# First pairs' queries and keys loaded in 96 rows of six tokens and turned on TensorE, with a bound on outstanding loads

## The chip, the core and the metric

The program runs on one core of a Trainium2 chip. It uses all five engines of the core: TensorE (PE in the profile, with its weight loads as PEld), VectorE (DVE), ScalarE (ACT), GpSimd (POOL) and SyncE (SP), which here only issues DMA transfers. The metric is the device time of one execution in microseconds. The kernel before takes 704.54 us (median of 3 runs, 704.47 to 704.87).

## The reference

Eight batches, eight heads, 576 tokens of 64 numbers. Attention has two parts that are added: one on sequences pooled by four (144 tokens), one local, in which a token sees those less than four places away. The result is the input of a gated feed-forward block.

```python
q_d, k_d, v_d = (mean over groups of 4 tokens)
out_up = repeat(softmax(q_d k_d^T / 8) v_d, 4)
scores = where(|i - j| < 4, q k^T / 8, -1e9)
x = out_up + softmax(scores) v              # to (8, 576, 512)
x_prev = x shifted by one token
xk = mu_k * x + (1 - mu_k) * x_prev         # and xr with mu_r
k = max(xk @ w_k, 0)                        # w_k 512 x 1024
v = k * k @ w_v                             # w_v 1024 x 512
out = sigmoid(xr @ w_r) * v                 # w_r 512 x 512
```

The weights come as 64-bit floats, all else as 32-bit floats.

## The kernel before, in words

**Attention** goes by pairs of heads: 32 pairs, four to a batch. Of a pair, queries and keys are loaded (`load_raw`, L328 to L338, four transfers each, of 32 partitions x 18 x 32 numbers, so runs of 32 numbers), values once for the pooled part (`load_v4`) and once as windows of 32 tokens for the local part (`load_windows`). `turn_q` (L372) and `turn_k` (L381) put the 64 numbers of each head on partitions with VectorE's 32x32 transpose, GpSimd pools by four (`pool_q`, `pool_k`, `pool_v` at L422), TensorE makes all scores of the pair in one PSUM tile `ps_a` of which there is one (`score_both`: `down_last`, `score_pe`, `down_pe`). Then follow maxima and sums on VectorE (L523 the pooled part's maximum, L466 or L472 the local one's), exponentials on ScalarE, normalising on GpSimd (L477, L492, L544), a turn of the local part on VectorE (`score_turn`, L497), its spreading into a block pattern `bd` on ScalarE (L503), a turn of the pooled part on TensorE (`down_turn`, L556 to L558, copied by L565), the products with the values (`av_pe`, L575 and L581), and the sum of both parts into the batch's tile `xt` (`av_out`, L611). From pair 5 on the products with the values of the pair before are issued in the middle of a pair's scores (`run_pe`).

**Feed-forward** goes by 18 chunks of 256 tokens. Of a chunk the two mixed inputs are made (`diff` L632, `mix_part` L643 or L647, `mix_add` L657), each split in a high part (L661) and a low part (`mix_low`, L666, tile `xkl` or `xrl`), since products run in float32r in three passes high x high, high x low, low x high. Then come `k_pe` (L674, eight blocks of 12 products), the square on ScalarE and its split (L679 to L693), `r_pe` (L704) and `v_pe` (L719). Chunks 0 and 1 need only batch 0, so pairs 0 to 3; chunk 2 is the first that needs batch 1, pairs 4 to 7.

**Weights.** Twenty blocks of 128 x 512 64-bit numbers are loaded (`fetch_weight`, L278, 512 KB each) and made into 32-bit ones: one step on ScalarE (`weight_scale`, L283), three on VectorE (L287, L291, L296), a high part on ScalarE (L301) and a low part, of the first eight by TensorE (L307, L308) and ScalarE (L318), of the other twelve on GpSimd (`weight_low`, L323). Their order is k0 to k3, v0 to v3, k4 to k7, v4 to v7, r0 to r3.

**Order.** A planner (`Plan`) is given every task with its engine, a cost, a rank and the tiles it reads and writes; it walks through time with these costs and writes down an order for each engine, which the program then holds to. SyncE's loads are tasks like others, in one order, on one queue. The planner also puts filler products (`keep_warm`, L314, tile `ps_x`, results unused) where it expects TensorE to wait, up to a planned time `WARM1`. A load's end is counted on one of eight semaphores that take turns, so that a load waits for the end of the eighth-last one whatever else it waits for.

Of the kernel before, what the change touches and what calls it, by code (L numbers as in the profile page):

```python
# [32 lines left out]
SPLIT = 8  # L33
PEM = 4
# [10 lines left out]
class Plan:  # L45
# [8 lines left out]
    WARM0, WARM1, FILLER = 5.0, 100.0, 0.24  # L54
# [36 lines left out]
    def order(self):  # L91
# [126 lines left out]
def attention_moe(ctx: ExitStack, tc, q, k, v, mu_k, mu_r, w_k, w_v, w_r, band, ident, out):  # L218
# [108 lines left out]

    def load_raw(n, nm):  # L328
        b, p = divmod(n, NP)
        src = {"q": q, "k": k}[nm]  # L330
        raw = wp.tile([P, 18, 32], F32, tag="raw", name=nm + "raw", bufs=4)
        for e in range(2):
            for dh in range(2):
                o = 64 * e + 32 * dh
                nc.sync.dma_start(  # L335
                    raw[o:o + 32],
                    src[b, 2 * p + e].rearrange("(c t) (g d) -> t c g d", t=32, g=2)[:, :, dh, :])
        st.setdefault(n, {})[nm + "raw"] = raw  # L338
# [35 lines left out]
    def turn_k(n):  # L374
# [12 lines left out]
        d["k4"] = [(h, kz[h, e, 3:579]) for e, h in enumerate((slice(0, 64), slice(64, P)))]  # L387

# [336 lines left out]
    def store_out(c, t):  # L725
# [5 lines left out]
                     xkl=2, xrh=1, xrl=1, kk=2, kh=4, kl=4, sig=3, att=1))  # L731
# [69 lines left out]
    def weight(i):  # L801
# [102 lines left out]
    for c in range(NCH):  # L904
        while n <= NP * (segs(c)[-1][0] + 1):
            if n < n1:
# [6 lines left out]
                else:  # L913
                    add("PE", 3.3 if n < SPLIT else 2.85, at_run[n], run_pe, n, **join(av_of(n - 1), s))
# [24 lines left out]
    for t in emitted:  # L939
        in_order(t["f"], *t["args"])  # L940
# [40 lines left out]
```

## Time and profile before

| | |
|---|---|
| median of 3 runs | 704.54 us |
| profiled execution, its own time | 705.88 us |
| its span, first to last instruction | 703.9 us |
| busy share of the span: PE, DVE, ACT, POOL | 96%, 66%, 62%, 43% |
| first product of the feed-forward part (L674) | 73.97 us after the span's start |
| PE busy from 200 to 600 us | 397.66 of 400 us |
| packets of all transfers | 221849, 62.21 MB |

The profile is one execution. Its page and views give busy time by engine, groups of instructions by source line with the idle time ahead of them and what ended it ("<-"), and the chain of work that ended last. SPq rows are SyncE issuing transfers: the row's length is the time to issue, including a wait for a free semaphore, not the transfer. PEclk is the granted TensorE clock, 1.00 being full. Line numbers L... of the kernel before are those of the listing above; the changed kernel's lines are some 10 to 45 higher.

### The profile page before, as it was taken

Reading aid. Unit: us, or ns where it says so; the run is one execution under the profiler, and the core shown is the slowest. Engines: PE = TensorE matmul, PEld = TensorE weight load, DVE = VectorE, ACT = ScalarE, POOL = GpSimd, SP = SyncE. Lnnn points to the kernel's source line nnn. Section 1 sums busy time; section 2 is a strip of 40 time slices with the busy share of each in tenths; the row PEclk is TensorE's granted clock in tenths of the full one; section 3 lists DMA queues with packets and bytes.
Section 4 is the critical chain, followed back from the end, with each engine's and each line's share of the span. In section 5 each row is a group of like instructions: output and inputs, shape, how many; then the busy total and the mean of one; then the engine's idle time right before and its main releaser. Section 6 shows DMA issues by size and latency. Waiting matters only on the chain.

```text
span 703.9 us, 18635 instructions
## 1 busy us (share of the span) xinstructions
PE 674.1 (96%) x7467; PEld 576.9 (82%) x7467; DVE 465.5 (66%) x855; ACT 439.3 (62%) x1095; POOL 303.3 (43%) x374
## 2 busy tenths in 40 slices
PE   7888977999999999999999999999999999999997
PEld 5565866888888888888888888888888888988986
DVE  4778987659965977498753996488748963555111
ACT  3557864777757765667665667585758575744432
POOL 5535898656453646345341555455544521000000
PEclk9999998999999999999999999999999999999999
DMA  8899997635353426242351364334351100000000
GB/s 149 181 197 273 221 148 132 124 79 116 68 114 75 107 56 128 54 93 44 87 87 52 59 115 88 88 77 104 71 101 40 53 2 31 1 30 31 1 32 31
DMA packets 221849, 62.21 MB, mean 88 GB/s; under 512 B 205122, under 2 KB 214594, under 8 KB 221762
## 3 DMA queue, kind: packets, MB, share of 16 engines
q1 hardware_dynamic: 221762, 61.01, 42.0%
q8 instruction: 59, 0.97, 0.6%
q14 instruction: 28, 0.23, 0.1%
HBM read 51.55 MB, written 9.44 MB: 87 GB/s over the span
## 4 chain that ended last, share of the span: by engine, by line
PE 69%; DVE 11%; ACT 5%; SPq 4%; POOL 4%; DMA 3%; issue 3%; DVEq 0%; POOLq 0%; ACTq 0%
PE ps_g L674 24%; PE acc L719 22%; PE ps_r L704 12%; PE ps_v L581 3%; SPq L335 3%; PE ps_a L449 2%; PE ps_v L575 2%; DMA v<-in_v_dram 1%; ACT ad L533 1%; ACT L533 1%; DVE ps_w L291 1%; PE ps_a L516 1%; DMA wv<-in_moe_w_v_dram 1%; DVE kl L693 1%; PE ps_a L509 1%
## 5 line engine op out<-in xcount | busy, mean ns | idle before, releaser
L674 PE MATMUL ps_g<-xkh,wk 128*128 128x256 f32 x1152 | 229.5, 285 | 2.9 <-ACT kk L679 2.0
L674 PEld LDWEIGHTS ps_g<-xkh,wk 128*128 128x128 f32 x1152 | 186.6, 190 | 11.4 <-ACT kk L679 4.9
L719 PE MATMUL acc<-wv,kh 128*128 128x512 f32 x576 | 181.2, 396 | 0.0
L674 PE MATMUL ps_g<-xkl,wk 128*128 128x256 f32 x576 | 162.6, 282 | 0.7 <-DVE xkl L666 0.7
L693 DVE TENSOR_TENSOR kl<-kk,kh 128x256 fp32r<-128x256 f32 x119 | 64.0, 538 | 118.0 <-ACT kh L686 110.8
L719 PEld LDWEIGHTS acc<-wv,kh 128*128 128x128 f32 x576 | 101.0, 189 | 18.9 <-issue 2.5
L674 PEld LDWEIGHTS ps_g<-xkl,wk 128*128 128x128 f32 x576 | 109.9, 191 | 3.9 <-DVE xkl L666 0.9
L719 PE MATMUL acc<-wv,kl 128*128 128x512 f32 x288 | 112.6, 391 | 0.1
L679 ACT ACTIVATE kk<-ps_g 128x256 f32<-128x256 f32 x144 | 54.5, 379 | 84.2 <-PE ps_g L674 77.9
L704 PE MATMUL ps_r<-wr,xrh 128*128 128x512 f32 x288 | 90.2, 394 | 1.7 <-POOL wr L323 1.4
L693 POOL TENSOR_TENSOR kl<-kk,kh 128x256 fp32r<-128x256 f32 x25 | 18.5, 742 | 124.2 <-PE acc L719 96.1
L719 PEld LDWEIGHTS acc<-wv,kl 128*128 128x128 f32 x288 | 54.1, 188 | 12.8 <-DVE kl L693 0.8
L686 ACT ACTIVATE kh<-kk 128x256 fp32r<-128x256 f32 x144 | 60.2, 418 | 4.6
L685 ACT ACTIVATE kk<-kk 128x256 f32<-128x256 f32 x144 | 60.1, 418 | 4.5
L704 PEld LDWEIGHTS ps_r<-wr,xrh 128*128 128x128 f32 x288 | 52.5, 188 | 12.4 <-POOL wr L323 1.8
L477 POOL TENSOR_TENSOR sm<-sm,mx 128x384 f32<-128x384 f32 x28 | 24.4, 873 | 83.1 <-DVE sd L539 60.6
L704 PE MATMUL ps_r<-wr,xrl 128*128 128x512 f32 x144 | 56.1, 390 | 0.0
L523 DVE TENSOR_REDUCE mxd<-ps_a 128x3 f32<-128x432 f32 x32 | 19.3, 604 | 48.8 <-PE ps_a L449 39.6
L422 POOL TENSOR_TENSOR v<-v 72x512 f32<-72x512 f32 x32 | 44.6, 1395 | 16.0 <-DMA v<-in_v_dram 15.8
L423 POOL TENSOR_TENSOR vd<-v 72x256 f32<-72x256 f32 x32 | 27.7, 866 | 51.0 <-PE ps_v L575 49.6
L413 POOL TENSOR_TENSOR tk<-kz 64x288 f32<-64x288 f32 (+1 forms) x56 | 41.9, 748 | 16.1 <-DVE kz L386 12.5
L533 ACT ACTIVATE ad<-ps_a,mxd 128x144 f32<-128x144 f32 x96 | 35.3, 376 | 20.3 <-DVE mxd L524 17.5
(106 smaller groups left out, 1212.5 us busy)
## 6 DMA issues: line engine op xcount, KB each, us to landing
vw<-in_v_dram SPq DMA_DIRECT2D x126, 96.0 KB
qraw<-in_q_dram SPq DMA_DIRECT2D x128, 72.0 KB
kraw<-in_k_dram SPq DMA_DIRECT2D x128, 72.0 KB
v<-in_v_dram SPq DMA_DIRECT2D x32, 288.0 KB
out_dram<-sig SPq DMA_DIRECT2D x36, 256.0 KB
wk<-in_moe_w_k_dram SPq DMA_DIRECT2D x8, 512.0 KB
wv<-in_moe_w_v_dram SPq DMA_DIRECT2D x8, 512.0 KB
wr<-in_moe_w_r_dram SPq DMA_DIRECT2D x4, 512.0 KB
```

The costliest lines, as they stand in the source:

```text
L413: nc.gpsimd.tensor_tensor(out=tk[h], in0=k4[:, :, 0:2], in1=k4[:, :, 2:4], op=ALU.add)
L422: eng.tensor_tensor(out=v4[:, :, 0:128], in0=v4[:, :, 0:128], in1=v4[:, :, 128:256], op=ALU.add)
L423: eng.tensor_tensor(out=vd, in0=v4[:, :, 0:64], in1=v4[:, :, 64:128], op=ALU.add)
L477: nc.gpsimd.tensor_tensor(out=s3, in0=s3, in1=mx[:, :, None].broadcast_to([P, 12, 32]), op=ALU.subtract)
L533: nc.scalar.activation(ad[:, t, :], ps[:, t, :], AF.Exp, scale=1.0 / 128, bias=mx[:, t:t + 1], accum_out=sd[:, t:t + 1])
L674: nc.tensor.matmul(ps, w_k_part(p, f, w), y[:, p, :], start=(m == 0), stop=(m == len(mm) - 1))
L679: nc.scalar.activation(kk, kq[c, f], AF.Relu)
L685: nc.scalar.activation(kk, kk, AF.Square)
L686: nc.scalar.activation(kh, kk, AF.Copy)
L693: eng.tensor_tensor(out=kl, in0=kk, in1=kh.bitcast(F32), op=ALU.subtract)
L704: nc.tensor.matmul(ps, y[:, p, P * t:P * t + P], ws[f"r{p}"][:, w, :], start=(m == 0), stop=(m == len(mm) - 1))
L719: nc.tensor.matmul(accs[c][t], x[:, P * t:P * t + P], ws[f"v{f}"][:, w, :], start=(f == 0 and m == 0), stop=(f == NF - 1 and m == 2))
```

## The change

- Queries and keys of pairs 0 to 3 (`n < LONG`) are loaded by two transfers each instead of four, into a tile of 96 partitions, six consecutive tokens on each, the two heads side by side (runs of 64 numbers). The tile lies in the buffers of the first chunks' `xkh` and `xkl`.
- These are turned on TensorE, six transposes of 96 x 128 for queries and six for keys (`turn_pe`), three to a PSUM bank, and each three copied out by one instruction, for queries on ScalarE, for keys on VectorE (`turn_copy`). VectorE's 32x32 transposes of these pairs go. Two new rings bound how many turns (`turn`) and weights (`slot`) are in the works.
- Until a planned time of 130, a load waits until all loads have ended that lie further back than some 4 planned microseconds of transfers (`landed_before`); the planner starts none more than 3 ahead of its transfers (`AHEAD`). Fillers are put in until 130 instead of 100.
- For pairs 5 to 7 scores and the products with the values of the pair before are two tasks, scores first.
- As costs and tasks differ, the planner's order differs on all engines in the first part of the program. After its first 500 or so of some 3300 rows TensorE's order is the same as before.

```diff
-    WARM0, WARM1, FILLER = 5.0, 100.0, 0.24
+    WARM0, WARM1, FILLER = 5.0, 130.0, 0.24
+    AHEAD = 3.0
+    QUEUE = 4.0
...
             s = max(ready_at[t["id"]], free.get(t["eng"], 0.0), held.get(t["lock"], 0.0))
+            if t["dma"]:
+                s = max(s, dma_free - self.AHEAD)
...
     def load_raw(n, nm):
         b, p = divmod(n, NP)
         src = {"q": q, "k": k}[nm]
+        if n < LONG:
+            raw = wp.tile([TP, TN, 2, D], F32, tag=early_home(nm), name=nm + "raw", bufs=2)
+            for e in range(2):
+                nc.sync.dma_start(raw[:, :, e, :], bass.AP(src.tensor, (b * H + 2 * p + e) * S * D,
+                                                           [[TN * D, TP], [D, TN], [1, D]]))
+            st.setdefault(n, {})[nm + "raw"] = raw
+            return
...
+    def turn_pe(n, nm, i):
+
+        raw, c0 = st[n][nm + "raw"], sum(HALF[:i])
+        ps = pp.tile([P, HALF[i], TP], F32, tag=plan.bank[f"t{nm}{n}.{i}"], name="ps_q", bufs=1)
+        for c in range(HALF[i]):
+            nc.tensor.transpose(ps[:, c, :], raw[:, c0 + c, :, :].rearrange("p e d -> p (e d)"), idn[0:TP, 0:TP])
+        st[n][nm + "turn", i] = ps
+
+    def turn_copy(n, nm, i):
+        d = st[n]
+        c0 = sum(HALF[:i])
+        to = qTs[n % 2][:, 0:576] if nm == "q" else kzs[n % 2][:, 0, 3:579]
+        to = to.rearrange("p (t c) -> p c t", c=TN)[:, c0:c0 + HALF[i], :]
+        if on_turn(nm, i) == "ACT":
+            nc.scalar.activation(to, d[nm + "turn", i], AF.Copy)
+        else:
+            nc.vector.tensor_copy(out=to, in_=d[nm + "turn", i])
...
-                    add("PE", 3.3 if n < SPLIT else 2.85, at_run[n], run_pe, n, **join(av_of(n - 1), s))
+                    if n < SPLIT:
+                        add("PE", 1.9, at_run[n], score_both, n, **s)
+                        add("PE", 1.6, at_run[n], av_pe, n - 1, **av_of(n - 1))
+                    else:
+                        add("PE", 2.85, at_run[n], run_pe, n, **join(av_of(n - 1), s))
...
+    def landed_before(t):
+
+        if plan.when[t["id"]][0] > plan.WARM1:
+            return None
+        work = 0.0
+        for x in reversed(sent):
+            work += x["dma"]
+            if work > plan.QUEUE:
+                return x["last"]
+        return None
...
+                if waits is not None and ins.engine == every[-1]:
+                    tc.add_manual_dep(ins, waits.name, mybir.DependencyInfo(
+                        mybir.DependencyClass.Sync, mybir.DependencyReason.DATA), reason="landed")
+                    waits = None
```

**SyncE, the first loads.** `qraw` and `kraw` are the tiles of queries and keys, `wk` blocks of the first weight, `vw` the windows of the values; DMAHW0 to DMAHW7 are the eight semaphores on which loads' ends are counted. Before, from the second weight block to the third:

```order
L278 DMA wk1_110<-in_moe_w_k_dram 128x1024 [waits DMAHW3_49]
L344 DMA v4_112<-in_v_dram 72x4x256 [waits DMAHW4_49]
L335 DMA qraw_115<-in_q_dram 32x18x32 [waits DMAHW5_49]
L335 DMA qraw_115<-in_q_dram 32x18x32 [waits DMAHW6_49]
L335 DMA qraw_115<-in_q_dram 32x18x32 [waits DMAHW7_49]
L335 DMA qraw_115<-in_q_dram 32x18x32 [waits DMAHW0_49]
L335 DMA kraw_126<-in_k_dram 32x18x32 [waits DMAHW1_49]
L335 DMA kraw_126<-in_k_dram 32x18x32 [waits DMAHW2_49]
L335 DMA kraw_126<-in_k_dram 32x18x32 [waits DMAHW3_49]
L335 DMA kraw_126<-in_k_dram 32x18x32 [waits DMAHW4_49]
L358 DMA vw_215<-in_v_dram 32x11x64 [waits DMAHW5_49]
L362 DMA vw_215<-in_v_dram 29x64 [waits DMAHW6_49,DVE_49]
```

and now:

```order
L288 DMA wk1_100<-in_moe_w_k_dram 128x1024 [waits DMAHW3_49]
L364 DMA v4_112<-in_v_dram 72x4x256 [waits DMAHW5_49,DMAHW0_49]
L347 DMA qraw_126<-in_q_dram 96x6x64 [waits DMAHW6_49,DMAHW1_49]
L347 DMA qraw_126<-in_q_dram 96x6x64 [waits DMAHW2_49]
L347 DMA kraw_140<-in_k_dram 96x6x64 [waits DMAHW7_49]
L347 DMA kraw_140<-in_k_dram 96x6x64 [waits DMAHW4_49]
L378 DMA vw_218<-in_v_dram 32x11x64 [waits DMAHW0_49]
L382 DMA vw_218<-in_v_dram 29x64 [waits DVE_49]
L378 DMA vw_218<-in_v_dram 32x12x64 x2
L378 DMA vw_218<-in_v_dram 32x12x64 [waits DMAHW1_49]
L288 DMA wk2_236<-in_moe_w_k_dram 128x1024 [waits DMAHW4_49,DMAHW2_49]
```

Eight issues for the second pair's queries and keys have become four, and rows name a second semaphore, that of a load which must have ended: the pair's queries now wait for the first weight block (DMAHW6), the third weight block for the pair's keys (DMAHW4).

**VectorE, around the first chunk's inputs.** `w32` is a weight in 32 bits, `xk32` the mixed input, `xkl` its low part, without which the first product of the chunk cannot run. Before:

```order
L287 TENSOR_SCALAR ps_w_985<-ps_w_985 128x512
L291 SCALAR_TENSOR_TENSOR ps_w_985<-wk6_532,ps_w_985 128x512
L296 SCALAR_TENSOR_TENSOR w32_1007<-wk6_532,ps_w_985 128x512
L287 TENSOR_SCALAR ps_w_995<-ps_w_995 128x512
L291 SCALAR_TENSOR_TENSOR ps_w_995<-wk7_536,ps_w_995 128x512
L296 SCALAR_TENSOR_TENSOR w32_1017<-wk7_536,ps_w_995 128x512
L657 TENSOR_TENSOR xk32_1010<-xk32_1010,xt_102 128x1024
L287 TENSOR_SCALAR ps_w_1005<-ps_w_1005 128x512
L291 SCALAR_TENSOR_TENSOR ps_w_1005<-wv4_609,ps_w_1005 128x512
L296 SCALAR_TENSOR_TENSOR w32_1033<-wv4_609,ps_w_1005 128x512
L666 TENSOR_TENSOR xkl_1036<-xk32_1010,xkh_1028 128x1024
L372 STREAM_TRANSPOSE qT0_76<-qraw_650 128x576
```

and now:

```order
L306 SCALAR_TENSOR_TENSOR w32_987<-wk5_781,ps_w_977 128x512
L297 TENSOR_SCALAR ps_w_981<-ps_w_981 128x512
L301 SCALAR_TENSOR_TENSOR ps_w_981<-wk6_799,ps_w_981 128x512
L392 STREAM_TRANSPOSE qT0_76<-qraw_954 128x576
L700 TENSOR_TENSOR xk32_989<-xk32_989,xt_102 128x1024
L306 SCALAR_TENSOR_TENSOR w32_1009<-wk6_799,ps_w_981 128x512
L401 STREAM_TRANSPOSE kz0_73<-kraw_970 128x576
L709 TENSOR_TENSOR xkl_1018<-xk32_989,xkh_1012 128x1024
L297 TENSOR_SCALAR ps_w_1007<-ps_w_1007 128x512
L700 TENSOR_TENSOR dx_979<-dx_979,xt_102 128x1024
L301 SCALAR_TENSOR_TENSOR ps_w_1007<-wk7_816,ps_w_1007 128x512
L306 SCALAR_TENSOR_TENSOR w32_1112<-wk7_816,ps_w_1007 128x512
```

Blocks wk7 and wv4 have moved behind `xkl`, and the turns of pair 4's queries and keys (`qT0`, `kz0`) from behind it to ahead of it.

**TensorE, pair 6 and the first gate product.** `ps_a` are scores, `ps_v` products with the values, `ps_r` the gate products `r_pe`, `ps_x` fillers. Before:

```order
L704 MATMUL ps_r<-wr_1559,xrh 128x512 x2
L704 MATMUL ps_r<-wr_1559,xrl 128x512
L704 MATMUL ps_r<-wr_1601,xrh 128x512 x2
L704 MATMUL ps_r<-wr_1601,xrl 128x512
L509 MATMUL ps_a<-kd,qd_69 128x144
L575 MATMUL ps_v<-adT,vd 64x144 x4
L581 MATMUL ps_v<-bd,vw 64x48 x24
L516 MATMUL ps_a<-kd,qd_69 64x144 x4
L454 MATMUL ps_a<-kz_73,qT_76 32x32 x48
L674 MATMUL ps_g<-xkh,wk_235 128x256
```

and now:

```order
L601 MATMUL ps_t<-idn,ad 72x2x16
L324 MATMUL ps_x<-nidn 128x512 x14
L552 MATMUL ps_a<-kd,qd_69 128x144
L497 MATMUL ps_a<-kz_73,qT_76 32x32 x48
L559 MATMUL ps_a<-kd,qd_69 64x144 x4
L618 MATMUL ps_v<-adT,vd 64x144 x4
L624 MATMUL ps_v<-bd,vw 64x48 x24
L747 MATMUL ps_r<-wr_1450,xrh 128x512 x2
L747 MATMUL ps_r<-wr_1450,xrl 128x512
L747 MATMUL ps_r<-wr_1608,xrh 128x512 x2
L747 MATMUL ps_r<-wr_1608,xrl 128x512
```

The scores of pair 6 now stand whole and ahead of pair 5's products with the values, both ahead of the gate products, and 14 fillers ahead of them.

More of the change, by code (lines that the diff above doesn't have):

```diff
@@ L33 @@
 SPLIT = 8
+LONG = 4
+SLOTS = 2
+TURNB = 2
+HALF = (3, 3)
+TP, TN = 96, 6
+TURNS = "AADD"
 PEM = 4
@@ L326, in attention_moe, with early_home @@
     st, xts = {}, {}
+    def early_home(nm):
+        return "xkh" if nm == "q" else "xkl"
     def load_raw(n, nm):
@@ L730, in attention_moe @@
     plan = Plan(dict(raw=4, v4=2, vw=3, kd=2, sm=2, ad=1, adT=1, at=1, up=2, vd=2, xt=2, f32tmp=2, xkh=2,
[L731 removed]
+                     xkl=2, xrh=1, xrl=1, kk=2, kh=4, kl=4, sig=3, att=1, slot=SLOTS, turn=TURNB))
     add = plan.add
@@ L758, in pair_scores @@
         if part == 0:
-            add("DVE", 0.77, R - 9, turn_q, n, r=[f"qraw{n}"], w=[f"qT{i}"])
+            if n < LONG:
+                for nm in "qk":
+                    for x in range(2):
+                        add("PE", 0.14 * HALF[x] + 0.1, R - 10, turn_pe, n, nm, x, r=[f"{nm}raw{n}", "idn"],
+                            new=[(f"t{nm}{n}.{x}", "bank"), (f"u{nm}{n}.{x}", "turn")])
+                for nm in "qk":
+                    for x in range(2):
+                        add(on_turn(nm, x), 0.18 * HALF[x] + 0.14, R - 9, turn_copy, n, nm, x, r=[f"t{nm}{n}.{x}", f"u{nm}{n}.{x}"],
+                            w=[f"{nm}T{i}" + (f".{x}" if 0 else "")])
+            else:
+                add("DVE", 0.77, R - 9, turn_q, n, r=[f"qraw{n}"], w=[f"qT{i}"])
             if SPLIT <= n < SPLIT + 2:
                 add("POOL", 0.5, R - 9, clear_plane, i, w=[f"kT{i}"])
-            add("DVE", 0.77 if n < SPLIT else 1.53, R - 8.5, turn_k, n, r=[f"kraw{n}"], w=[f"kT{i}"])
+            if n >= LONG:
+                add("DVE", 0.77 if n < SPLIT else 1.53, R - 8.5, turn_k, n, r=[f"kraw{n}"], w=[f"kT{i}"])
             add("POOL", 1.12, R - 7, pool_q, n, r=[f"qT{i}"], w=[f"qd.{i}"])
@@ L922, in attention_moe, with in_order @@
     emitted = plan.fill(plan.order(), keep_warm)
-    last = {}
-    def in_order(f, *args):
+    last, sent = {}, []
+    def landed_before(t):
[7 more added lines that the diff above has]
+        return None
+    def in_order(f, *args, waits=None):
         traced = nc.cur_bb.bb.instructions
@@ L939, in attention_moe @@
     for t in emitted:
-        in_order(t["f"], *t["args"])
+        if t["eng"] == "SP":
+            in_order(t["f"], *t["args"], waits=landed_before(t))
+            sent.append(dict(dma=t["dma"], last=last[every[-1]]))
+        else:
+            in_order(t["f"], *t["args"])
 _INS = ["q", "k", "v", "moe_mu_k", "moe_mu_r", "moe_w_k", "moe_w_v", "moe_w_r"]
```

14 lines of the change are left out of this document (10 added, 4 removed).

## The prediction

> **What bounds the kernel now.** I read the view by stages first: busy microseconds of each engine in stretches, granted clock, share of the sixteen DMA engines.
>
> ```profile
> core 0: us, PE busy (x) PEld busy (x) DVE busy (x) ACT busy (x) POOL busy (x), PEclk, DMA share, GB/s
> 0.00:20.00 20.00, 14.36 (x152) 9.92 (x153) 9.59 (x20) 7.63 (x19) 11.01 (x28) 1.00 0.81 150
> 20.00:40.00 20.00, 17.81 (x373) 12.53 (x372) 12.53 (x27) 8.69 (x27) 9.81 (x14) 1.00 0.84 164
> 40.00:60.00 20.00, 14.92 (x219) 9.89 (x217) 15.89 (x34) 12.37 (x35) 7.52 (x10) 1.00 1.07 233
> 60.00:80.00 20.00, 18.98 (x137) 15.46 (x138) 18.99 (x25) 16.93 (x35) 12.74 (x10) 0.91 1.04 293
> 80.00:100.00 20.00, 18.34 (x272) 15.77 (x273) 18.69 (x31) 16.93 (x47) 19.28 (x23) 1.00 1.14 153
> 100.00:120.00 20.00, 13.23 (x290) 10.28 (x289) 13.62 (x22) 8.39 (x25) 16.84 (x18) 0.90 0.76 121
> 120.00:140.00 20.00, 19.76 (x287) 17.39 (x279) 13.86 (x28) 14.43 (x36) 13.18 (x18) 0.93 0.66 133
> 200.00:600.00 400.00, 397.66 (x4497) 346.26 (x4489) 278.39 (x522) 262.65 (x662) 175.58 (x213) 1.00 0.36 75
> ```
>
> From 120 us on TensorE never stops (397.66 of 400 us), and there its order is the same in both kernels. So whatever moves the start of that part moves the end by as much. The start is another matter: TensorE's first product of the feed-forward part waits, and its busy time before that is largely filler:
>
> ```profile
> 63.52 10.53 PE L314 MATMUL ps_x<-nidn 128*128 128x512 f32 x43
> 75.01 0.38 PE L674 MATMUL ps_g<-xkl,wk 128*128 128x256 f32 x1 [0.69 <-DVE xkl L666]
> ```
>
> VectorE sets that start: 18.99 and 18.69 of 20 us busy from 60 to 100, but only 38.01 of the first 60. What it waits for stands in its groups up to 125 us (busy, mean ns | idle ahead, what ended it):
>
> ```profile
> L287 DVE TENSOR_SCALAR ps_w<-ps_w 128x512 int32<-128x512 int32 x20 | 13.8, 689 | 9.2 <-ACT ps_w L283 9.2
> L372 DVE STREAM_TRANSPOSE qT<-qraw 128x576 f32<-128x576 f32 x9 | 7.0, 776 | 6.1 <-DMA qraw<-in_q_dram 6.0
> L381 DVE STREAM_TRANSPOSE kz<-kraw 128x576 f32<-128x576 f32 x8 | 6.1, 764 | 1.2 <-DMA kraw<-in_k_dram 1.2
> L611 DVE TENSOR_TENSOR xt<-ps_v,up 128x288 f32<-128x288 f32 x12 | 4.8, 443 | 0.0
> L523 DVE TENSOR_REDUCE mxd<-ps_a 128x3 f32<-128x432 f32 x7 | 4.2, 604 | 8.0 <-PE ps_a L454 4.8 <-PE ps_a L516 3.2
> L497 DVE STREAM_TRANSPOSE at<-sm 128x384 f32<-128x384 f32 x6 | 3.4, 571 | 2.6 <-POOL sm L492 2.6
> ```
>
> The 9.2 us at L287 are weights that had not landed; two of the waits are
>
> ```profile
> 25.41 0.70 DVE L287 TENSOR_SCALAR ps_w<-ps_w 128x512 int32<-128x512 int32 x1 [3.86 <-ACT ps_w L283]
> 46.70 0.70 DVE L287 TENSOR_SCALAR ps_w<-ps_w 128x512 int32<-128x512 int32 x1 [2.03 <-ACT ps_w L283]
> ```
>
> Last the chain of waits over the first 145 us, by line, and the queue:
>
> ```profile
> by line: SPq L335 13.9%; issue 8.4%; DMA v<-in_v_dram 6.7%; DVE ps_w L291 4.2%; DMA wv<-in_moe_w_v_dram 4.1%; DVE ps_w L287 3.7%; DMA wk<-in_moe_w_k_dram 3.5%; SPq L358 3.1%; PE ps_g L674 2.8%; POOL v L422 2.6%; DMA vw<-in_v_dram 2.2%; POOL
> 1.64 2.04 SPq L335 DMA_DIRECT2D qraw<-in_q_dram  x4
> 3.73 2.12 SPq L335 DMA_DIRECT2D kraw<-in_k_dram  x4
> ```
>
> Issuing queries and keys (L335) is 13.9% of 145 us, 20 us, of the chain: more than any engine's work. So in the first 60 us loads bound, from 60 to 100 VectorE (with GpSimd at 19.28 of 20 from 80), then TensorE.
>
> **The change part by part**, each in microseconds of the end; the sum goes from the profiled execution's own 705.88.
>
> *Loads, +5.0.* A load of queries or keys takes SyncE 2.04 to 2.12 when nothing holds it, 0.52 an issue; with two issues 1.04. That is 4.2 less ahead of the weight awaited at 25.41 (four such loads) and 8.3 less ahead of the one awaited at 46.70 (eight). In packets the load goes from 2304 of 128 bytes to 1152 of 256.
>
> ```profile
> q1 hardware_dynamic: 221762, 61.01, 42.0%
> ```
>
> 42.0% of 16 engines over 703.9 us for 221762 packets is 21.3 ns each, at a mean of 275 bytes. If cost goes by packet, a load falls from 3.07 to 1.53 us of the sixteen engines, 12.3 for eight; if by byte, nothing. VectorE can win at most its 9.2 at L287, and nothing if the loads go by bytes and its own order keeps it waiting elsewhere (8.0 at L523 is for scores, which stays). I take 5.0: the 3.86 and 2.03, covered by 4.2 and 8.3, less one.
>
> By the Trainium skill ("DMA: Bandwidth & Descriptors", Why small descriptors are slow) a descriptor has an overhead of about 3 cycles beside one per 32 bytes: 7 cycles for 128 bytes, 11 for 256. By it, an estimate, a load keeps 79% of its engine time, nearer to the byte end than to the packet end.
>
> *First pair, +0.5.* The waits at L372 and L381 (7.3 in all) start the chain. Keys need 1.04 less of issuing in each of two loads, but turn and copy come between: six transposes at the pace of
>
> ```profile
> 19.07 0.30 PE L556 MATMUL ps_t<-idn,ad 128*72 128x128 f32 x1 [1.04 <-POOL ad L544]
> 19.64 0.26 PE L558 MATMUL ps_t<-idn,ad 128*72 128x32 f32 x2
> ```
>
> are 0.8, two copies 0.7 to 0.9 in place of a turn of 0.77. Bounds -0.5 to 1.5.
>
> *VectorE's work, +2.6.* Four turns of queries go, 4 x 0.776 = 3.1. Four of keys, 3.06, become eight copies from PSUM; nearest is L611, 288 numbers from PSUM in 0.443: 3.54. Net 2.6. The copies write with a stride of six; at twice the price it would be -0.9.
>
> *ScalarE, 0.* Eight copies like
>
> ```profile
> 43.45 0.41 ACT L565 ACTIVATE adT<-ps_t 72x288 f32<-72x288 f32 x1 [1.04 <-PE ps_t L558]
> ```
>
> are 3.3 us, hidden: ScalarE is busy 16.3 of the first 40. Without that cover, -3.3. TensorE's 48 transposes, about 6 us, stand where fillers did.
>
> *Pair 3's values, +1.0.* They land late, with GpSimd and then the turn waiting:
>
> ```profile
> 55.81 1.27 POOL L422 TENSOR_TENSOR v<-v 72x512 f32<-72x512 f32 x1 [1.90 <-DMA v<-in_v_dram]
> 58.71 0.58 DVE L497 STREAM_TRANSPOSE at<-sm 128x384 f32<-128x384 f32 x1 [1.29 <-POOL sm L492]
> ```
>
> With less ahead of them they come earlier; 0 to 1.3, I take 1.0.
>
> *Order, 0.* Blocks wk7 and wv4 go behind `xkl`: six steps, 6 x 0.69 = 4.1, off the first product, but owed to the weights after it; pair 4's two turns, 1.54, go ahead. That moves the first product, not the end. Splitting scores from the products with the values frees VectorE's wait at `ps_a L454`, up to 4.8; against it stand 18 fillers behind the first products, 18 x 0.245 (10.53 by 43) = 4.4, free only while TensorE waits there, which it does now (100 to 120: 6.77 idle). I take 0 of -4.4 to 4.8.
>
> *Landing waits, -1.5.* SyncE issues in order, so each holds all later loads. A wait costs what the loads in flight do not cover:
>
> ```profile
> 1.17 0.42 SPq L240 DMA_DIRECT2D idn<-in_ident_dram  x1
> 3.12 0.31 ACT L247 ACTIVATE nidn<-idn 128x128 fp32r<-128x128 f32 x1 [1.11 <-DMA idn<-in_ident_dram]
> 60.00:64.00 4.00, 3.67 (x53) 2.36 (x54) 3.69 (x7) 3.96 (x9) 0.20 (x1) 0.67 1.03 411
> ```
>
> From issue to use 1.95 us; a weight of 512 KB at 411 GB/s is 1.28. With one weight in flight the queue runs dry for 0.67, with two not at all. Most places keep two or three; the third weight block and the values behind it keep one. I take 1.5, of 0 to 0.67 for each of some 34 loads.
>
> **Sum.** 5.0 + 0.5 + 2.6 + 0 + 1.0 + 0 - 1.5 = 7.6: 705.88 becomes 698.3. The median lay 1.34 below that execution, so 696.9; I say 697. The first product should come at 75.0 - 7.6 - 4.1 + 1.5, about 65.
>
> **The rivals.**
>
> *More is won (692.5).* The idle 6.77 from 100 to 120 and the clock of 0.90 there also go: the split run lets scores pass and fillers keep the clock, 4.5 more. For it: the chain's 8.4% "issue". Against it: GpSimd is at 16.84 of 20 there, and the last weight's low part is late on it:
>
> ```profile
> 112.36 1.27 POOL L323 TENSOR_TENSOR wr<-w,wr 128x512 fp32r<-128x512 f32 x1
> ```
>
> *Given back at GpSimd (702).* Its work is not reduced, and at 19.28 of 20 it takes over: only VectorE's 2.6 remains at the end, though the first product comes early. Against it: GpSimd idles 7.26 from 60 to 80, so it too can start earlier.
>
> *Packets cost by the byte (701).* The change then does not do what it says: the loads' 5.0 fall to some 1 by SyncE alone. For it: the DMA share is 1.04 to 1.14 from 40 to 100. Against it: 0.81 and 0.84 in the first 40, where these loads are.
>
> *The landing waits starve the queue (709).* The place is SyncE's queue from the second weight on. If each of some 34 loads up to wv7 is late by 0.4, 13.6 is lost against 9.1 won, 4.5 slower; from 0.27 each it ends slower. Pair 4's queries are behind all these, and their turn now stands ahead of `xk32` on VectorE, so the first product would be held directly. Against it: loads waited before too, for the eighth-last, and that covers little less for runs of small ones. The Trainium skill's same page (Anatomy of one DMA) puts the fixed cost of a transfer near 2 us, most of it the receipt after the last byte, written for transfers that GpSimd issues; the 1.95 here agrees, and it is the reason why a wait for the landing is dear.
>
> **How the numbers follow.** Forecast 0.52, more 0.13, GpSimd 0.12, by the byte 0.11, starved 0.12. The forecast's own range, with its terms' half-way bounds, is 693 to 700.5; with the rivals 690 to 704, which leaves out the starved case and a part of "more". A measurement here tells 0.2% or 1.4 us from no change. Of the middle cases at 701 and 702 a fifth may end within that: same 0.07; slower 0.11; faster 0.82.
>
> **What would show it.** Right: L287's idle time in VectorE's groups falls from 9.2 to about 4; queries and keys take SyncE about 1.0 a load; the first `ps_g` product near 65; VectorE's busy time in the first 60 us at 43 or more of 60; TensorE from 200 to 600 unchanged. Wrong: SPq rows of 2 us and more that wait for loads while the DMA share from 20 to 60 falls below 0.8 (starved); a first product near 65 but TensorE's idle time from 75 to 120 up by 5 (given back); loads that land no sooner (by the byte).

## Result: 0.6% slower

The changed kernel takes 709.72 us (median of 16 runs, 705.21 to 712.42) against 705.9 for the kernel before, measured beside it: a ratio of 1.0059, 95% interval 1.0043 to 1.0075. The forecast was 697 with a range of 690 to 704. The changed kernel's profiled execution took 708.9 us, with a span of 707.0.

The view by stages of the changed kernel, with the columns of the one shown for before:

```profile
0.00:20.00 20.00, 12.30 (x154) 9.00 (x154) 8.81 (x18) 9.25 (x22) 11.15 (x28) 1.00 0.72 171
20.00:40.00 20.00, 15.79 (x280) 11.73 (x279) 13.45 (x28) 12.20 (x32) 10.77 (x16) 0.94 0.82 188
40.00:60.00 20.00, 16.07 (x308) 10.79 (x308) 12.57 (x30) 9.97 (x28) 5.69 (x7) 0.93 0.77 207
60.00:80.00 20.00, 18.24 (x142) 14.80 (x141) 17.45 (x25) 14.24 (x30) 11.53 (x9) 0.96 0.91 253
...
200.00:600.00 400.00, 397.37 (x4512) 345.94 (x4511) 279.46 (x522) 261.99 (x660) 176.23 (x213) 1.00 0.36 75
```

From 200 us on nothing has changed (397.37 of 400 busy, 397.66 before). The loss is in the first part: VectorE is busy 34.83 of the first 60 us, less than the 38.01 of before and not the 43 hoped for, and the DMA share from 40 to 60 has gone from 1.07 to 0.77. So VectorE waits more than before, and the transfer engines are not full.

What SyncE's queue waits for in the first 76 us (waiting line, what it waits for, us in total, times, longest), first in the kernel before, then in the changed one:

```profile
SPq L335 <- DMA wk<-in_moe_w_k_dram: 2.6, 3, 1.0
...
SPq L278 <- DMA v<-in_v_dram: 1.4, 1, 1.4
SPq L344 <- DMA wv<-in_moe_w_v_dram: 1.4, 1, 1.4
```

```profile
SPq L288 <- DMA wk<-in_moe_w_k_dram: 6.6, 4, 3.6
SPq L347 <- DMA wk<-in_moe_w_k_dram: 5.0, 3, 2.4
SPq L288 <- DMA wv<-in_moe_w_v_dram: 4.3, 2, 3.4
```

These are single waits of 2.4 to 3.6 us for a landing, the first half of the sign that the prediction gave for the starved queue; the DMA share from 20 to 60, the other half, is 0.80 and lies at the bound of 0.8 that it set. What the waits do to the weights stands in the order of time on that queue (start, us from the first issue's start to the last one's end, number of issues), before and then changed:

```profile
42.70 1.86 SPq L278 DMA_DIRECT2D wv<-in_moe_w_v_dram  x3
46.00 0.32 SPq L344 DMA_DIRECT2D v<-in_v_dram  x1
...
49.93 6.16 SPq L278 DMA_DIRECT2D wk<-in_moe_w_k_dram  x4
56.46 2.52 SPq L278 DMA_DIRECT2D wv<-in_moe_w_v_dram  x4
59.72 7.15 SPq L335 DMA_DIRECT2D qraw<-in_q_dram  x4
```

```profile
40.65 2.64 SPq L288 DMA_DIRECT2D wv<-in_moe_w_v_dram  x3
44.34 0.32 SPq L364 DMA_DIRECT2D v<-in_v_dram  x1
48.15 1.86 SPq L378 DMA_DIRECT2D vw<-in_v_dram  x4
52.56 3.85 SPq L288 DMA_DIRECT2D wk<-in_moe_w_k_dram  x4
60.11 4.08 SPq L288 DMA_DIRECT2D wv<-in_moe_w_v_dram  x4
66.23 2.43 SPq L355 DMA_DIRECT2D qraw<-in_q_dram  x4
```

At 40 us the changed kernel is ahead by 2 (42.70 against 40.65 for the same three weights); at 60 it is 3.7 behind (56.46 against 60.11), and 6.5 at pair 4's queries. Between the rows are gaps in which nothing is sent: 44.7 to 48.15, 50.0 to 52.56, 56.4 to 60.11. The first feed-forward product that needs `xkl` follows:

```profile
76.71 0.39 PE L717 MATMUL ps_g<-xkl,wk 128*128 128x256 f32 x1 [1.76 <-DVE xkl L709]
```

It starts at 76.71, where it started at 75.01 before and forecast at 65, though six steps of weight work were moved behind it.

VectorE's groups up to 125 us show where it now idles:

```profile
L297 DVE TENSOR_SCALAR ps_w<-ps_w 128x512 int32<-128x512 int32 x20 | 13.8, 691 | 6.9 <-ACT ps_w L293 6.9
L425 DVE COPY kz<-ps_q 128x288 f32<-128x288 f32 x8 | 4.8, 666 | 8.8 <-PE ps_q L414 8.7
L654 DVE TENSOR_TENSOR xt<-ps_v,up 128x288 f32<-128x288 f32 x12 | 4.8, 441 | 4.0 <-ACT up L646 4.0
L540 DVE STREAM_TRANSPOSE at<-sm 128x384 f32<-128x384 f32 x6 | 3.5, 575 | 5.1 <-POOL sm L535 5.0
```

The wait for weights fell from 9.2 to 6.9 only; the wait for the first pair is 8.8 where it was 7.3; a copy takes 666 ns, not 443; and waits for ScalarE (`up`, 4.0) and GpSimd (`sm`, 5.0) are new or larger.

### The profile page after: what moved, and what is told of

The parts are those of the page before. It is cut to its first block, busy times and chain, and to the rows that moved or that the text cites. A ratio compares the mean times of both kernels' runs of the same rounds, so it can differ in the third digit from the quotient of the medians.

```text
span 707.0 us, 18679 instructions
## 1 busy us (share of the span) xinstructions
PE 675.9 (96%) x7501; PEld 580.2 (82%) x7501; DVE 464.7 (66%) x855; ACT 443.4 (63%) x1103; POOL 302.8 (43%) x374
## 4 chain that ended last, share of the span: by engine, by line
PE 75%; DMA 10%; DVE 5%; ACT 4%; POOL 2%; SPq 2%; issue 1%; DVEq 0%; ACTq 0%; POOLq 0%
PE ps_g L717 26%; PE acc L762 24%; PE ps_r L747 13%; PE ps_v L624 3%; PE ps_a L492 3%; DMA wk<-in_moe_w_k_dram 2%; PE ps_v L618 2%; DMA wv<-in_moe_w_v_dram 2%; DMA vw<-in_v_dram 2%; DMA kraw<-in_k_dram 1%; SPq L355 1%; ACT ad L576 1%; PE ps_a L559 1%; DMA qraw<-in_q_dram 1%; ACT L576 1%
## 5 line engine op out<-in xcount | busy, mean ns | idle before, releaser
L736 DVE TENSOR_TENSOR kl<-kk,kh 128x256 fp32r<-128x256 f32 x119 | 65.8, 553 | 120.6 <-ACT kh L729 114.3
L466 POOL TENSOR_TENSOR vd<-v 72x256 f32<-72x256 f32 x32 | 26.1, 816 | 49.9 <-PE ps_v L618 48.5
```

The source lines that it names most:

```text
L466: eng.tensor_tensor(out=vd, in0=v4[:, :, 0:64], in1=v4[:, :, 64:128], op=ALU.add)
L736: eng.tensor_tensor(out=kl, in0=kk, in1=kh.bitcast(F32), op=ALU.subtract)
```

## The experiments

All ratios are to the kernel before, measured beside each kernel, with 95% intervals. Unless a fence says so, "no waits" means the changed kernel without its landing waits, whose order of instructions on every engine is that of the changed kernel. The expectations name three theories: A, the landing waits starve the queue; B, the copies and the later first pair cost the time; C, the new order costs it.

**Landing waits away (`e1_no_wait`).**

```
 def landed_before(t):
-    if plan.when[t["id"]][0] > plan.WARM1:
-        return None
+    return None
```

> The changed kernel without the landing waits; on every engine its instructions stand in the same order as in the changed kernel, and the loads wait only for the eighth-last, as before. Kernel before: 705.9; changed kernel: 709.7. If the landing waits starve the queue (theory A), they are the whole loss and most of the gain comes back: 698 to 703, the weight awaited at about 60 us issued 4 us earlier, DMA share from 40 to 60 back at 1.0 or more. If the copies from PSUM and the later first pair cost the time (B: 666 ns a copy where 443 was forecast, first scores 1.3 us later): within 1 us of 709.7. If the new order costs it (C: split run, fillers, weights moved behind the first products): also within 1 us of 709.7.

Measured 704.45 us, 0.9976 [0.9957, 0.9995]. From 1.0059 that is 0.8%, some 5.9 us, for the waits alone, so they are the whole loss, as A says. But 704.45 misses A's own 698 to 703: only 1.7 us are left as a gain, where the forecast without its term for the waits was 9.1. The queue is full again, and VectorE's wait for weights falls nearly as far as forecast, while its wait for the first pair stays. By stages (the same columns), and then what VectorE waits for up to 76 us:

```profile
40.00:60.00 20.00, 16.94 (x297) 12.33 (x298) 15.82 (x34) 12.23 (x34) 5.42 (x6) 1.00 1.02 293
80.00:100.00 20.00, 17.36 (x252) 15.01 (x251) 17.14 (x28) 16.72 (x43) 19.39 (x22) 1.00 1.02 138
100.00:120.00 20.00, 17.94 (x231) 14.59 (x230) 17.95 (x33) 10.39 (x31) 17.32 (x20) 0.91 0.66 100
```

```profile
DVE kz L425 <- PE ps_q L414: 8.0, 1, 8.0
DVE ps_w L297 <- ACT ps_w L293: 5.3, 7, 1.7
...
DVE xt L654 <- ACT up L646: 2.3, 1, 2.3
```

The first `xkl` product comes at

```profile
72.50 0.39 PE L717 MATMUL ps_g<-xkl,wk 128*128 128x256 f32 x1 [1.39 <-DVE xkl L709]
```

4.2 before the changed kernel's. The first 60 us as a whole, in the kernel before and then without waits:

```profile
0.00:60.00 60.00, 47.09 (x741) 32.34 (x741) 38.00 (x79) 28.69 (x78) 28.34 (x51) 1.00 0.91 183
```

```profile
0.00:60.00 60.00, 45.99 (x768) 33.26 (x770) 39.26 (x80) 34.16 (x89) 28.35 (x51) 0.97 0.96 231
```

VectorE is busy 39.26 where the prediction asked for 43: what it waits less for weights it waits more for other things, the first pair and ScalarE's `up` among them. GpSimd has done 51 pieces and 28.3 us of work in both.

**Landing waits alone, on the kernel before (`e3_wait_alone`).** The changed kernel's `landed_before`, with the old layout and order.

> The kernel before with the landing waits alone: old layout, and on every engine the old order. Theory A (waits starve the queue): 709 to 712, slower than 705.9 by 3 to 6, since the 34 loads up to the last weight block are each held as in the changed kernel. B (copies) and C (order): 705 to 707, no change.

709.5 us, 1.0048 [1.0032, 1.0065]. That is A again, in its range: 3.4 us with the old order, where loads wait for the eighth-last as well.

**The bound at 8.0 and at 2.0 (`e2_queue8`, `e21_queue2`).** One number, same order; the second kernel has 2.0 there:

```
-    QUEUE = 4.0
+    QUEUE = 8.0
```

> The changed kernel with the bound on loads outstanding at 8.0 us of the planner's transfer time in place of 4.0; order on every engine as in the changed kernel. With 4.0 the ratio to the kernel before was 1.0059, without landing waits 0.9976. If each wait costs what the loads in flight fail to cover, twice as many in flight cover nearly all: 0.997 to 1.000, 704 to 706. If a wait for a landing costs by itself, however early the load was sent: 1.003 to 1.006, 708 to 710.

> The changed kernel with the bound on loads outstanding at 2.0 in place of 4.0, same order. Ratios so far: 8.0 gives 0.9959, 4.0 gives 1.0059. If a wait costs what the loads in flight do not cover, one load in flight leaves the queue dry after each: 0.67 more for each of some 34 loads, up to 20 us, 1.015 to 1.04. If each wait has a fixed price that 4.0 already paid in full: 1.005 to 1.009.

8.0: 702.89 us, 0.9959 [0.9943, 0.9975]. 2.0: 755.09 us, 1.0698 [1.0674, 1.0721]. So 8.0 costs nothing (0.997 to 1.000 was expected), 4.0 costs 0.8%, and 2.0 costs 7%, more than the 4% at most that was expected: a wait costs what the transfers in flight do not cover, and it is no fixed price. From 20 to 60 us the transfer engines' share is 0.98 without waits, 0.80 at 4.0 and 0.59 at 2.0. The rows are of the kernel without waits, the changed one, and the one at 2.0 (share: last but one):

```profile
20.00:60.00 40.00, 33.22 (x615) 24.40 (x616) 29.86 (x63) 24.89 (x67) 17.28 (x24) 0.96 0.98 248
```

```profile
20.00:60.00 40.00, 31.86 (x587) 22.52 (x586) 26.03 (x58) 22.17 (x60) 16.46 (x23) 0.94 0.80 198
```

```profile
20.00:60.00 40.00, 30.09 (x521) 21.84 (x519) 21.32 (x46) 18.80 (x49) 14.49 (x21) 0.83 0.59 158
```

The kernel with 8.0 beats both kernels. That it is also better than no waits at all is not shown: the intervals overlap.

**Old layout, the rest of the change kept (`e5_old_layout`), and without waits (`e6_order_alone`).**

```
-LONG = 4
+LONG = 0
```

> The changed kernel with the old layout for all pairs; landing waits, split run, planner's bound on transfers and fillers stay. Theory A: 710 to 714, the waits' loss without the layout's gain. B: 705 to 706, as before, since the copies are gone. C: 709 to 711, the order's loss alone.

> The changed kernel without landing waits and with the old layout: only the planner's new rules (split run, fillers to 130 us, bound on transfers in the plan) against the kernel before; on every engine the order is that of the old-layout kernel that took 1.0082 with the waits. With the new layout these rules gave 0.9976; there 128-byte packets cost 0.9%. If the new layout is worth its packets here too: 1.003 to 1.008. If the order itself gains and the layout adds little (its later first pair and dearer copies eat the packets' gain): 0.996 to 1.000, as with the new layout. By the landing waits' price with the old order (0.48%) taken off 1.0082: 1.003.

With waits 712.17 us, 1.0082 [1.0061, 1.0104], in A's range; without 704.08 us, 0.9971 [0.9957, 0.9986]. The waits cost 1.1% here. The second number says more: with the planner's new rules and no waits the old layout is not told apart from the new one (0.9976). So what is won over the kernel before comes with the order, and no gain of the layout is seen at the end. Where the waits make loads late it may help (1.0082 to 1.0059), but those intervals overlap.

**The layout alone (`e4_layout`).** No waits, no split run, no bound on transfers in the plan, old number of fillers.

> The kernel before with the layout of the first four pairs alone (two issues a load, six transposes, two copies), planned by the old rules: no landing waits, no bound in the planner on transfers, no split run of scores and products with the values, old number of fillers. Theory A: faster, 699 to 703 (less issuing on SyncE, nothing held). B: 708 to 710, slower than 705.9 by the later first pair and the dearer copies. C: 702 to 705, a little faster, since the layout does no harm.

708.43 us, 1.0048 [1.003, 1.0067], in B's range, but for another reason. This plan sends eleven weight blocks in a row ahead of pair 3's values, which go at 54.39 us, 8.4 later than before, and TensorE runs dry while VectorE works on those weights. SyncE's queue in order of time, and the stage:

```profile
42.82 3.26 SPq L288 DMA_DIRECT2D wv<-in_moe_w_v_dram  x4
47.63 6.67 SPq L378 DMA_DIRECT2D vw<-in_v_dram  x4
54.39 0.39 SPq L364 DMA_DIRECT2D v<-in_v_dram  x1
```

```profile
60.00:80.00 20.00, 10.69 (x179) 7.73 (x178) 17.45 (x30) 12.42 (x29) 14.72 (x15) 0.50 0.93 195
```

It was busy 10.69 of 20 at a granted clock of 0.50. So this measures that order, not the layout; the pair above, in which the same rules made both plans, is the better comparison.

**Four issues a load, and small packets (`e16_issues4`, `e17_packets128`).** No waits, all orders but SyncE's the same. The first sends each head's load in two halves of the tokens, the second in two halves of each row:

```
 for e in range(2):
-    nc.sync.dma_start(raw[:, :, e, :], ...)
+    for x in range(2):
+        nc.sync.dma_start(raw[:, 3 * x:3 * x + 3, e, :], ...)
```

```
 for e in range(2):
-    nc.sync.dma_start(raw[:, :, e, :], ...)
+    for x in range(2):
+        nc.sync.dma_start(raw[:, :, e, 32 * x:32 * x + 32], ...)
```

> The changed kernel without landing waits, each load of queries or keys of the first four pairs sent in four issues instead of two, with the same 256-byte packets; all other engines in the same order. If issuing on SyncE was what the new layout saved (about 0.5 to 0.6 for each issue, 16 issues more): 707 to 710, ratio 1.002 to 1.006. If packets were what it saved, or if neither sets the end: 704 to 705.5, ratio 0.997 to 0.999.

> As the kernel with four issues for each load, but each issue takes half of every row, so that the packets are of 128 bytes again, 2304 for a load as in the kernel before. If the cost goes by the packet (21 ns each, 1.5 us of the sixteen engines for a load, 12 for eight): slower than four issues with 256-byte packets by 3 to 6, 708 to 714. If it goes by the byte: the same as that kernel within 1 us.

Four issues: 705.16 us, 0.9994 [0.9974, 1.0015], not told apart from two. Small packets: 711.96 us, 1.0082 [1.0057, 1.0107], 0.9% on top. So dearer loads do reach the end. That small packets cost nothing in the old layout (0.9971), whose order was planned for them, and 0.9% here, where the order was planned for large ones, was not taken apart. Two stretches with hardly a packet of a weight give a packet's price: queue, number of packets, MB, share of the sixteen engines from 16 to 20 us, with 256 and then with 128 bytes:

```profile
q1 hardware_dynamic: 1618, 0.40, 43.5%
```

```profile
q1 hardware_dynamic: 3100, 0.39, 63.0%
```

43.5% of 64 us of engine time is 27.8 for 1618 packets, 17.2 ns each; 63.0% is 40.3 for 3100, 13.0 each. A load of 1152 large packets takes 1.24 us of the sixteen engines, one of 2304 small ones 1.87: it keeps 66%, so neither by packet (50%) nor by byte (100%). Each price is from one stretch of one execution: in the kernel before, 3528 packets from 4 to 8 us, nearly all of 128 bytes, took 83.3%, 15.1 each, and by that the load keeps 57%. By the Trainium skill ("DMA: Bandwidth & Descriptors", Why small descriptors are slow) the estimate in the prediction was 79%; these rows make the gain of larger descriptors greater than that.

**First pair in the old layout (`e23_pair0_old`); all copies on VectorE, in token order (`e24_dddd`).** No waits; the first planned anew, the second with the copies written as in the next experiment.

```
-if n < LONG:
+if 1 <= n < LONG:
```

```
-TURNS = "AADD"
+TURNS = "DDDD"
```

> The changed kernel without landing waits, with the first pair in the old layout and only pairs two to four in the new one (planned anew by the new rules). New layout for all four: 0.9976; old for all: 0.9971. If the first pair's longer way (first scores up to 1.3 us later, VectorE waiting 8.0 us for it) eats the packets' gain: 0.994 to 0.996. If the price lies in every pair (copies on ScalarE, transposes in TensorE's queue): 0.996 to 0.999.

> The changed kernel without landing waits, with all sixteen copies on VectorE, in token order (442 ns each there), so that ScalarE has none (its eight took 706 ns each, and VectorE waited 2.3 us for an activation behind them). If ScalarE's copies are the price: 0.993 to 0.996. If VectorE's own work sets the end: eight more copies at 0.44 are 3.5 us, 1.000 to 1.003. If neither: 0.996 to 0.999.

704.04 us, 0.9982 [0.9968, 0.9995], and 703.29 us, 0.9967 [0.9947, 0.9987]. Neither is told apart from 0.9976: the first pair's longer way and ScalarE's copies are seen in the waits, and no cost of theirs is seen at the end.

**Copies in token order (`e18_token_order`).** Bound at 8.0.

```
-to = to.rearrange("p (t c) -> p c t", c=TN)[:, c0:c0 + HALF[i], :]
+to = to.rearrange("p (t c) -> p t c", c=TN)[:, :, c0:c0 + HALF[i]]
+got = d[nm + "turn", i].rearrange("p c t -> p t c")
```

> The kernel with the bound at 8.0 (0.9959), with the sixteen copies walking PSUM and the tiles token by token, three neighbours at a time written side by side, and 96 numbers apart read, where they were read side by side and written six apart; same order and results. If the stride of the writes made a copy 666 ns in place of the 443 forecast: copies fall to 450 to 550, the first pair and VectorE win 1 to 2 us, 0.993 to 0.995. If the number of pieces or the read from PSUM sets it: 660 to 700 ns and 0.995 to 0.998.

703.36 us, 0.9974 [0.9954, 0.9994]. A copy falls to the duration that the prediction had taken:

```profile
L426 DVE COPY kz<-ps_q x8: 398/448/468, 10.1 to 37.6; 128x288 f32<-128x288 f32 x8
```

(shortest, median and longest ns; 615/678/705 without waits and with the old writes.) Some 1.8 us less on VectorE move nothing that can be seen.

**The old layout with the bound at 8.0, and the free parts together (`e25_q8_old_layout`, `e28_pair0_q8_tok`).**

> Old layout, new planner's rules, and the bound on loads outstanding at 8.0: the same order as the old-layout kernel without landing waits (0.9971). In the new layout 8.0 gave 0.9959 against 0.9976 without. If the milder bound gains by itself (transfers in flight share the engines less): 0.994 to 0.996. If it is only free: 0.996 to 0.999. If the old layout's larger loads (four issues, 2304 packets) make it bind: 0.999 to 1.003.

> The parts that should be free or better, together: first pair in the old layout, pairs two to four in the new one with copies in token order, bound on loads outstanding at 8.0, new planner's rules. If first pair and stride each cost something: 0.991 to 0.995, the fastest so far. If loads do not set the end in any of these: 0.995 to 0.998, like the others.

704.07 us, 0.9977 [0.9964, 0.999], and 703.27 us, 0.9972 [0.9959, 0.9984]. The same again. But in the first of the two the first `xkl` product comes 7.0 us earlier than in the kernel before:

```profile
68.05 0.39 PE L717 MATMUL ps_g<-xkl,wk 128*128 128x256 f32 x1 [0.79 <-DVE xkl L709]
```

The end comes some 1.5 us earlier. Of the 6.2 us that TensorE waits for other engines from 68 to 140 us, 5.4 are for GpSimd.

**Loads far cheaper (`e29_runs1536`).** No waits; six tokens of a head are one packet, and twelve products with the unit matrix turn them.

```
-raw = wp.tile([TP, TN, 2, D], F32, ...)
+raw = wp.tile([TP, 2, TN, D], F32, ...)
-for e in range(2): nc.sync.dma_start(raw[:, :, e, :], ...)
+nc.sync.dma_start(raw.rearrange("p e c d -> p e (c d)"),
+                  bass.AP(src.tensor, (b * H + 2 * p) * S * D, [[TN * D, TP], [S * D, 2], [1, TN * D]]))
-nc.tensor.transpose(ps[:, c, :], raw[:, c0 + c, :, :].rearrange("p e d -> p (e d)"), idn[0:TP, 0:TP])
+for e in range(2):
+    nc.tensor.matmul(ps[64 * e:64 * e + 64, c, :], raw[:, e, c0 + c, :], idn[0:TP, 0:TP], ...)
```

> The changed kernel without landing waits, the first pairs' queries and keys loaded in packets of 1536 bytes (six tokens of one head in a row: 192 packets and one issue a load in place of 1152 and two), turned by twelve products of 64 columns with the unit matrix in place of six transposes of 128. Same order on every engine. If loads or their issue set the end: 3 to 6 us faster than the 704.5 without landing waits, 0.988 to 0.993. If the loads do not set it any more: 0.996 to 0.999, and only waits at the weights fall.

705.75 us, 0.9996 [0.9974, 1.0018]. VectorE's wait for weights up to 76 us falls to

```profile
DVE ps_w L297 <- ACT ps_w L293: 2.4, 4, 1.0
```

from 8.9 in the kernel before, and no gain is seen in the time. Once the landing waits are away, loads cheaper than these win nothing, though dearer ones (the small packets above) still cost.

**GpSimd's late work doubled (`e31_pool_twice`).** No waits; the low parts of the last eight weight blocks are computed twice, to the same result.

```
+for _ in range(2 if i >= 12 and i not in LOWDVE else 1):
     eng.tensor_tensor(out=lo, in0=part32[i], in1=hi.bitcast(F32), op=ALU.subtract)
```

> The changed kernel without landing waits, GpSimd making the low parts of the last eight weight blocks twice (8 times 1.3 us, 10.4 more on GpSimd between some 80 and 130 us; the same result twice). If GpSimd sets the start of TensorE's part (the rival in which the gain is given back at GpSimd): 6 to 10 us slower than 704.5, 1.006 to 1.012. If VectorE sets it: 0 to 2 us, 0.997 to 1.001.

713.12 us, 1.0091 [1.0064, 1.0119]: 1.15%, or 8.1 us, slower than without waits for 10.4 us of work; the two intervals make it 6 to 10 us. The group of the last four blocks on GpSimd from 60 to 140, eight for four:

```profile
L334 POOL TENSOR_TENSOR wr<-w,wr 128x512 fp32r<-128x512 f32 x8 | 10.2, 1281 | 0.3
```

The first product has not moved (72.6 here, 72.5 without the doubling), so the loss lies behind it. Without waits and without doubling, the chain of waits from 95 to 140 us reads

```profile
by line: issue 9.6%; POOL tq L440 6.9%; PE ps_r L747 6.7%; POOL wr L333 5.7%; POOL v L465 5.5%; POOL tk L456 5.0%; POOL ad L587 4.0%; PE acc L762 3.8%; POOL sm L535 3.5%; POOL vd L466 3.2%; PE ps_g L717 3.2%; DVE w L306 3.1%; DVE mxd L567 3
```

The GpSimd pieces named there are 33.8%, TensorE's 13.7%. So GpSimd has some 2 us to spare there, hardly more, and it sets the start of TensorE's part or helps to set it. The same amount of work added to VectorE or ScalarE in that stretch was not tried.

**No split run; old number of fillers (`e7_no_split`, `e8_warm100`).** No waits. The first makes one run of scores and products with the values again and is planned anew; the second is

```
-WARM0, WARM1, FILLER = 5.0, 130.0, 0.24
+WARM0, WARM1, FILLER = 5.0, 100.0, 0.24
```

> The changed kernel without landing waits and without the split run: scores of a pair and products with the values of the pair before go as one run again, replanned by the otherwise new rules. Without landing waits the ratio was 0.9976. If the split run is where the order's gain comes from (VectorE's wait at the scores up to 4.8 us): 1.001 to 1.005. If it moves only waits that something else then ends: 0.996 to 0.999.

> The changed kernel without landing waits, and with fillers planned up to 100 us as before, not 130: 18 fillers of 0.245 us fewer behind the first products of the feed-forward part; all other instructions in the same order. Without landing waits alone: 704.5, ratio 0.9976. If the fillers stand in the way of work, 4.4 us are won: 0.991 to 0.994, 700 to 702. If they fill only time in which TensorE waits anyway: unchanged, 0.996 to 0.999. If they hold the clock up (0.90 granted from 100 to 120 us in the kernel before): slower, 0.999 to 1.003.

No split: 705.16 us, 1.0004 [0.9986, 1.0023]; against 0.9976 the split may be worth some 0.3%, but the intervals overlap. Without the late fillers: 706.65 us, 1.0012 [0.9995, 1.0029], 0.36% slower; the intervals only touch. Its row from 100 to 120, beside 17.94 busy at a clock of 0.91 with them:

```profile
100.00:120.00 20.00, 13.99 (x204) 11.03 (x204) 17.26 (x34) 9.60 (x26) 18.58 (x22) 0.74 0.84 123
```

That the fillers keep the granted clock up there is not shown by this pair of executions: the old-layout kernel with the landing waits has fillers in that stretch too (21 from 115.65 us on) and still 0.74, and the kernel before has none and 0.90. The two profiled executions end alike (span 702.8 both), so the difference is in the timed runs only, and its cause stays open.

## Why the prediction was wrong

Two of its rivals act here on top of each other: the starved queue is shown, the gain given back at GpSimd in part.

*The step that failed first: "Landing waits, -1.5".* The mechanism was named, and the term was mis-sized: taken at 1.5, it measured 5.9 with the new order (1.0059 against 0.9976) and 3.4 with the old (1.0048). The rival's 709 is the measured time by luck: it set 13.6 lost against 9.1 won, and 5.9 against 1.7 were measured. The working had a slip: it took the 1.95 from issue to use of a load of 64 KB and subtracted the 1.28 of transfer of a weight of 512 KB, which left 0.67. At the same 411 GB/s the 64 KB need only 0.16 of the 1.95, so by these rows some 1.8 come on top of the transfer, and a weight alone would take some 3.1, an estimate. The chains of waits show more still. The planner counts a weight as 1.75, so in a run of weights each waits for the last but one sent ahead of it at 2.0 (two in flight), for the last but two at 4.0 (three). One weight in the kernel with 2.0, then one in the changed kernel:

```profile
67.21 4.46 DMA wk<-in_moe_w_k_dram
```

```profile
53.75 6.34 DMA wk<-in_moe_w_k_dram
```

From 63 to 80 us the weights in the first chain take 4.0 to 4.5 each, from 53 to 66 us those in the second 3.7 to 6.3, none as little as 3.1. By our reading a load shares the engines with what else is in flight, so the load that a wait is on lands late while the rest runs out. Two weights in flight do not cover that, nor do three, as the dose shows: 8.0 free, 4.0 at 0.8%, 2.0 at 7%. A landing of this length already stood in the kernel before, in its own chain of waits:

```profile
39.98 5.96 DMA wv<-in_moe_w_v_dram
```

The argument against the rival, that loads waited before too for the eighth-last, was no protection: that wait is met by much older loads, and cost the queue single waits of 1.4 at most for landings.

*The step that failed second: that what VectorE wins before the first product moves the end.* Without the waits the sum was 9.1; measured were 1.7. Term by term:

- *Loads, +5.0.* Half of the mechanism held: the wait for weights went from 9.2 to 5.3, 3.9 less, where 5 was taken. SyncE's part was smaller, 1.31 to 1.36 for a load, not 1.04, because an issue became longer (0.62 in the median, 0.50 before); a load keeps 57 to 66% of its engine time. The other half failed: VectorE waits for other things instead, and in the first 60 us it is busy only 1.3 us more. Nor is any of it seen at the end: the old layout is as fast (0.9971), and loads of a sixth of the packets are no faster (0.9996).
- *First pair, +0.5.* Wrong in sign: VectorE waited 8.0 for it in place of 7.3. Also without an effect seen at the end (0.9982 with the first pair in the old layout).
- *VectorE's work, +2.6.* Only 0.8 was saved: eight copies of 666 ns take 5.3, not 3.54, since their writes are six apart. The prediction had named this as a bound at twice the price; one and a half times came. At the end no price is seen, as the copies in token order show.
- *ScalarE, 0.* Eight copies took 706 ns each, not 410, and VectorE waited 2.3 for `up` behind them; at the end nothing is seen of it (0.9967 with none of them).
- *Pair 3's values, +1.0.* They do come earlier: without waits GpSimd takes them up at 48.68 in place of 55.81 and waits 0.85 for them, not 1.90. What that is worth at the end was not measured.
- *Order, 0.* Here lies what was won: 0.9971 with the old layout, 2.0 us. The split may be a part of it. The 18 fillers, which the prediction held for a possible loss of 4.4, cost nothing: without them the time was 0.36% longer, at the edge of what these runs tell.

The rival "given back at GpSimd" gave 702 and 2.6 us of gain; without waits it came to 704.45 and 1.7, and 10.4 us more on GpSimd cost 8.1. Its argument in the prediction was GpSimd's 19.28 of 20 us from 80 to 100; against it stood that GpSimd idles from 60 to 80 and could start earlier. It hardly did: without waits it has done no more in the first 60 us than before (28.35 and 28.34), is at 14.17 of 20 from 60 to 80 where it was at 12.74, and again at 19.39 from 80 to 100. What it does late needs ScalarE's and VectorE's work on the same weights and pairs first, as its groups from 60 to 125 us show in the idle time ahead of them:

```profile
L440 POOL TENSOR_TENSOR tq<-qT 128x288 f32<-128x288 f32 x5 | 5.5, 1091 | 2.1 <-DVE qT L392 2.1
L333 POOL TENSOR_TENSOR wk<-w,wk 128x512 fp32r<-128x512 f32 x4 | 5.2, 1300 | 5.3 <-ACT wk L311 5.3
```

In that rival the first product should have been early and TensorE idle behind it; the product was early by 2.5 us only (72.50 against 75.01), so the sign that the prediction gave for this rival did not come in full. Part of that is order (VectorE had both of pair 4's turns ahead of it, and an `xkl` of 2.1 us in place of 1.2); the rest was not taken apart. In the old layout with the bound at 8.0 the product was early by 7.0 and the end by some 1.5, as that rival says. So the second step fails in two places: VectorE won little before the first product, and what a product comes earlier is mostly lost behind it. That GpSimd alone takes it there is argued from its row, the chain and the doubled work; it is not shown.

The forecast put 0.12 on each of these two rivals, and its main case counted gains on VectorE one for one although the row for GpSimd was already in front of it.

## What to carry to other kernels

A bound on outstanding transfers must hold more in flight than one loaded landing takes, read from the chain of waits under load (6 us here, not the 1.95 of a lone small load); try two values, since between 8.0 and 4.0 lay the whole loss of this kernel. Before a shorter wait is counted as a gain, look at what the engine waits for next, and at its busy time. Then look for the engine that is full right behind it and double its work: ten microseconds that cost eight say that it has no time to spare. And a layout change is only measured against the old layout under the same planner's rules; planned anew by other rules, it measures the order.

## What the runs showed of the hardware

- A copy of 288 numbers from PSUM took 678 ns on VectorE in the median when written six apart, and 448 when three neighbours were written side by side and the read was strided instead, so here the stride cost on the writing side. On ScalarE the same two forms took 706 and 463 in the mean.
- A packet of 128 bytes took 13.0 to 15.1 ns of an engine and one of 256 bytes 17.2. An issue of 96 x 6 x 64 numbers took SyncE 0.62 us in the median, one of 32 x 18 x 32 numbers 0.50.
- A weight of 512 KB took 4.0 to 4.5 us to land with two such loads in flight and 3.7 to 6.3 with three, though 512 KB at the 411 GB/s that the kernel before reached from 60 to 64 us are 1.28.
- The granted clock was 0.50 in a stretch where TensorE was busy 10.69 of 20 us. From 100 to 120 us it was 0.91 with and 0.74 without the 18 late fillers, one execution each; what sets it there is not shown.
